# One decode block on one core: query 0's first 24 keys loaded into the values' buffer, ahead of the first weights

## The chip, the cores and the metric

The kernel runs on one core of a Trainium2 chip. A core has five engines that work side by side: TensorE (PE, matrix multiplies), VectorE (DVE), ScalarE (ACT), GpSimd (POOL) and SyncE (SP), which here does nothing but issue transfers. Sixteen transfer (DMA) engines carry data between memory and the core's own buffers. The metric is the time of one execution in microseconds (us), as the median of several runs. Before the change it is 1301.37 us over three runs (1301.36 to 1301.38).

## The reference

One token for each of two batch entries goes through attention over a cache of 8192 keys and values, and then through a gated layer without a nonlinearity:

```python
# B = 2, D = 448, H = 16 heads, Sk = 8192, Dh = 256, F = 1792
h  = x + attention(layernorm(x), k_cache, v_cache, wq, wo)
#    q = layernorm(x) @ wq, split by head;  scores = q . k * Dh**-0.5
#    p = softmax(scores);  o = p @ v;  attention = o @ wo
n  = layernorm(h)
h2 = h + ((n @ w_gate) * (n @ w_up)) @ w_down
```

All is float32. There are 32 queries (16 heads by two batch entries), and each has 8.39 MB of keys and as much of values that no other query reads.

## The kernel before

The 8192 keys of a query lie on 128 partitions as 64 keys of 256 numbers each ("j" from 0 to 63 in the code). A transfer of all keys of a query is 128 rows of 64 KB. The buffer `k_sb` (line 245) has 112 such key slots: even queries take slots 0 to 63 and odd ones 48 to 111 (`k_base`, line 276), so the two overlap in 16 slots. The buffer `v_sb` (line 246) has 64 slots and holds the values of one query at a time. Its last two slots hold the input x at the start (line 263).

For each query VectorE multiplies the keys with the query in place (`scores`, line 451, `tensor_mul`) and reduces every key to one score (`tensor_reduce`), in two parts: 16 keys first, and then 48. For query 0 the parts are other ones: `FIRST` (line 22) names keys 40 to 63 (the "first 24 keys") and then keys 0 to 39. The products of the first part go to the start of `v_sb` and not back to `k_sb` (line 459). So slots 48 to 63 of `k_sb` come free for query 1's keys as soon as that multiply is done. VectorE then takes the maximum of the scores, TensorE and ScalarE make the softmax, and TensorE multiplies it with the values (`mix`, line 496).

At the very start TensorE turns x around, a layer norm is made of it, and 16 multiplies of two passes each (32 in the trace, name `q_ps<-w_sb,xb`) give the queries of heads 0 and 1 out of the first weights. They come in four groups of eight passes. Behind each group ScalarE copies one query (`q<-q_ps,rstd`). VectorE's first multiply needs the query of the first group.

All large transfers are issued by SyncE, in program order, and each is held back until the place that it writes is free. A list of accesses by buffer and range (`_needs`, line 112) works out which engine has to be waited for. The order at the start is: the weights `d_w0` (line 303), query 0's keys 40 to 63 and then 0 to 39 (lines 304 and 305), query 1's keys, query 0's values, query 2's keys, further weights, query 1's values. Query 0's values need `v_sb`, so they wait for the reduction of the first 24 keys. Query 2's keys need slots 0 to 63, so they wait until query 0's keys and the first 16 keys of query 1 are reduced.

Of the kernel before, what the change touches and what calls it, by code (L numbers as in the profile page):

```python
# [10 lines left out]
B, D, H, SK, DH, F = 2, 448, 16, 8192, 256, 1792  # L11
# [10 lines left out]
FIRST = ((NJ - AHEAD, NJ), (0, NJ - AHEAD))  # L22
# [193 lines left out]
def decode_block(nc, x, k_cache, v_cache, w, wg, wu, wd, out):  # L216
# [3 lines left out]
    def sb(name, *shape):  # L220
        return nc.alloc_sbuf_tensor(name, list(shape), F32)[:]
# [9 lines left out]
    def dve(method, *args, **kw):  # L231
        put("DVE", method, *args, **kw)
# [13 lines left out]
    v_sb = sb("v_sb", P, NJ, DH)  # L246
# [19 lines left out]
    def keys(cache, i, lo, hi):  # L266
        h, b = divmod(i, B)
        return cache[b, h].rearrange("(p j) d -> p j d", p=P)[:, lo:hi, :]

    def load_keys(name, cache, i, lo, hi, buf, at, event=None):  # L270
        o.load(
            "SP", name, buffers[buf][:, at : at + hi - lo, :], keys(cache, i, lo, hi),
            writes=[(buf, at * DH, (at + hi - lo) * DH)], event=event,
        )

    def k_base(i):
        return i % 2 * (NJ - OVER)

    def load_k(i, lo=0, hi=NJ):
        load_keys(f"d_k_{i}_{lo}", k_cache, i, lo, hi, "k", k_base(i) + lo)  # L280
# [13 lines left out]
    def load_w(name, k, lo, hi, event=None):  # L294
        o.load("SP", name, w_sb[:, lo:hi], w[k][:, lo:hi], writes=[("w", lo, hi)], event=event)
# [4 lines left out]
    def wo_at(h):  # L300
        return 2 * WQ + h % 4 * WO

    load_w("d_w0", 0, 0, WQ)
    for lo, hi in FIRST:
        load_k(0, lo, hi)

    ident = sb("ident", P, P)
    put("POOL", "memset", ident, 0.0, w=["ident"])
# [77 lines left out]
    def q_at(h):  # L386
        return h % 2 * (1 + h // 2 % 2)

    for k in range(2):
        for b in range(B):  # L390
            for c in range(DC):
                at = c * 2 * DH + (k * DH if c < DC - 1 else 0)
# [5 lines left out]
            at = q_at(k)  # L398
# [44 lines left out]
    def score_parts(i):  # L443
        if i == 0:
            return list(FIRST)
        at = [(k - 1) % (NJ // HC) * HC if i % 2 == 0 else k * HC for k in range(NJ // HC)]
        if i in FINE:
            return [(lo, lo + HC) for lo in at]
        return [(at[0], at[0] + HC), (at[1], at[1] + NJ - HC)]

    def scores(i, part, between=None):
        h, b = divmod(i, B)
        s, name = s_t[i % 2], f"s{i % 2}"
        lo, hi = score_parts(i)[part]
        at = k_base(i) + lo
        kt = k_sb[:, at : at + hi - lo, :]
        qk, there = kt, ("k", at * DH, (at + hi - lo) * DH)
        if i == 0 and part == 0:
            qk, there = v_sb[:, : hi - lo, :], ("v", 0, (hi - lo) * DH)
        q, slot = qs[b], q_at(h)  # L460
        here = ("k", at * DH, (at + hi - lo) * DH)
        dve(
            "tensor_mul", qk, kt, q[:, slot, :][:, None, :].to_broadcast([P, hi - lo, DH]),
            r=[here, (f"q{b}", slot, slot + 1)], w=[there],
        )
        if between is not None:
            between()
        dve("tensor_reduce", s[:, lo:hi], qk, axis=AX.X, op=ALU.add, r=[there], w=[(name, lo, hi)])
# [143 lines left out]
    for n in range(NQ + 1):  # L612
        hp, at = divmod(n, 2 * B)
# [3 lines left out]
        if n < NQ:  # L617
            scores(n, 0, (lambda: softmax(n - 1)) if n > 0 else None)
        else:
            softmax(n - 1)  # L620
# [8 lines left out]
        if n % 8 == 1:  # L629
            k = n // 8 + 1  # L630
# [5 lines left out]
        if n == NQ:  # L636
            norm_last()
        else:
            for part in range(1, len(score_parts(n))):
                scores(n, part, norm_last if part == 1 else None)  # L640
# [25 lines left out]
    at = 0  # L666
# [191 lines left out]
```

## Time and profile before

| | |
|---|---|
| median of three runs | 1301.37 us |
| span of the profiled execution, first to last instruction | 1300.5 us |
| what the timed median has beyond that span | 0.9 us |
| VectorE busy | 1130.8 us (87%) |
| TensorE busy | 488.8 us (38%) |
| moved by the transfer engines | 561.45 MB, 432 GB/s over the span |
| chain that ended last | DMA 70%, DVE 29% |

The page gives no time of the profiled execution other than its span. The span leaves out what lies ahead of the first instruction and behind the last one. The chain that ended last is followed back from the last instruction, at each step to what released it. A transfer is listed by its issue, with the time until it has landed, which includes its wait in the queue behind earlier transfers.

### The profile page before, as it was taken

What the parts mean: (1) busy time and instruction counts of PE and PEld (TensorE: products, weight loads), DVE (VectorE), ACT (ScalarE), POOL (GpSimd) and SP (SyncE); (2) the same over time, 40 slices, a digit from 0 to 9 for tenths busy, and PEclk for the clock granted to TensorE, in tenths of its full rate; (3) what the DMA queues carried; (4) which work ended last, traced back from release to release, by engine and by line L of the source; (5) the groups of instructions that cost most, each with busy time, mean ns of one, the idle gap of its engine ahead of it and who ended that gap; (6) DMA issues with size and microseconds to landing.
All of it is one profiled execution on the core that took longest, in us unless ns stands there. A gap on an engine that the chain in (4) does not pass through costs nothing.

```text
span 1300.5 us, 6955 instructions
## 1 busy us (share of the span) xinstructions
PE 488.8 (38%) x2972; PEld 168.9 (13%) x2972; DVE 1130.8 (87%) x275; ACT 62.6 (5%) x184; POOL 1.4 (0%) x9
## 2 busy tenths in 40 slices
PE   3035422363331633215343063432424334243368
PEld 2011100120100201002101021010111001010113
DVE  7996988888988689888889868898888897889991
ACT  1000000000000000000000000000000000000000
POOL 0000000000000000000000000000000000000000
PEclk8566756686656766558666576665766667666578
DMA  9999999999999999999999999999999999999998
GB/s 414 423 434 448 424 437 431 427 441 423 448 424 435 448 423 443 427 439 429 435 435 423 433 448 423 448 424 443 427 443 427 423 436 445 426 438 429 435 433 374
DMA packets 12111, 561.45 MB, mean 432 GB/s; under 512 B 1602, under 2 KB 1732, under 8 KB 1988
## 3 DMA queue, kind: packets, MB, share of 16 engines
q1 hardware_dynamic: 12096, 561.30, 99.8%
q8 instruction: 6, 0.10, 0.0%
q14 instruction: 5, 0.04, 0.0%
q10 hardware_dynamic: 4, 0.00, 0.0%
HBM read 561.19 MB, written 0.11 MB: 432 GB/s over the span
## 4 chain that ended last, share of the span: by engine, by line
DMA 70%; DVE 29%; PE 0%; issue 0%; SPq 0%
DMA k_sb<-in_A_k_cache_dram 68%; DVE k_sb L229 14%; DVE s L229 14%; DMA k_sb<-in_wd_dram 2%; DVE nm L229 0%; PE y_ps L229 0%; SPq L176 0%; DVE m L229 0%; PE sm L229 0%; DVE v_sb L229 0%; DVE rl L229 0%
## 5 line engine op out<-in xcount | busy, mean ns | idle before, releaser
L229 DVE TENSOR_TENSOR k_sb<-k_sb,q 128x12288 f32<-128x12288 f32 (+2 forms) x67 | 549.6, 8203 | 130.3 <-DMA k_sb<-in_A_k_cache_dram 130.3
L229 DVE TENSOR_REDUCE s<-k_sb 128x48 f32<-128x12288 f32 (+2 forms) x67 | 549.3, 8198 | 0.2
L229 PE MATMUL o_ps<-v_sb,p 128*2 128x512 f32 x2000 | 288.2, 739 | 397.7 <-PEq L183 387.6
L229 PEld LDWEIGHTS o_ps<-v_sb,p 128*2 128x2 f32 x2000 | 53.7, 97 | 603.8 <-issue 591.3
L229 PE MATMUL sm<-nm,ones 1*128 1x1 f32 x64 | 16.6, 326 | 191.7 <-PEq L183 175.1
L229 PE MATMUL sm<-ident,m 128*1 128x128 f32 x32 | 10.9, 341 | 137.0 <-PEq L183 106.1
L229 PE MATMUL q_ps<-w_sb,xb 128*128 128x256 f32 (+1 forms) x172 | 59.3, 503 | 0.0
L229 ACT ACTIVATE o_sb<-o_ps 128x512 f32<-128x512 f32 x32 | 19.1, 597 | 703.9 <-PE o_ps L229 703.9
L229 PE MATMUL sm<-sel,o_sb 128*128 128x1 f32 x256 | 33.7, 253 | 25.8 <-PEq L183 22.9
L229 PE MATMUL acc_ps<-w_sb,oT 128*2 128x448 f32 x60 | 36.6, 749 | 15.9 <-PEq L183 11.0
L229 PEld LDWEIGHTS sm<-nm,ones 1*128 1x128 f32 x64 | 14.6, 283 | 201.2 <-issue 183.5
L229 PEld LDWEIGHTS sm<-sel,o_sb 128*128 128x128 f32 x256 | 31.8, 195 | 55.6 <-issue 48.2
L229 PEld LDWEIGHTS q_ps<-w_sb,xb 128*128 128x128 f32 x172 | 33.7, 200 | 30.0 <-issue 27.6
L229 PE MATMUL sm<-lsum,ones 128*128 128x1 f32 x64 | 17.5, 342 | 26.0 <-PEq L183 23.1
L229 ACT ACTIVATE nb<-sm 128x1 f32<-128x1 f32 x32 | 5.5, 171 | 395.7 <-PE sm L229 395.7
L229 PEld LDWEIGHTS sm<-ident,m 128*1 128x1 f32 x32 | 2.6, 81 | 149.8 <-issue 115.3
L229 PEld LDWEIGHTS sm<-lsum,ones 128*128 128x128 f32 x64 | 15.6, 303 | 28.0 <-issue 24.7
L229 ACT ACTIVATE q<-q_ps,rstd 128x512 f32<-128x512 f32 (+1 forms) x18 | 11.5, 640 | 71.9 <-PE q_ps L229 71.9
L229 PE MATMUL o_ps<-k_sb,p 128*2 128x512 f32 x48 | 9.3, 934 | 6.1 <-DMA k_sb<-in_A_v_cache_dram 6.1
L229 ACT ACTIVATE p<-s,nb 128x64 f32<-128x64 f32 x32 | 11.1, 347 | 1.0
L229 DVE TENSOR_TENSOR v_sb<-k_sb,q 128x6144 f32<-128x6144 f32 x1 | 6.6, 6557 | 4.8 <-DMA k_sb<-in_A_k_cache_dram 4.8
L229 PE MATMUL q_ps<-k_sb,xr 128*32 128x256 f32 (+3 forms) x96 | 10.0, 506 | 1.6 <-DMA k_sb<-in_B_w_gate_dram 1.6
(79 smaller groups left out, 85.1 us busy)
## 6 DMA issues: line engine op xcount, KB each, us to landing
v_sb<-in_A_v_cache_dram SPq DMA_DIRECT2D x4, 4096.0 KB, 30.5
w_sb<-in_w_dram SPq DMA_DIRECT2D x3, 3584.0 KB, 37.8
v_sb<-in_A_v_cache_dram SPq DMA_DIRECT2D x1, 6144.0 KB, 24.3
k_sb<-in_A_k_cache_dram SPq DMA_DIRECT2D x1, 5120.0 KB, 24.6
v_sb<-in_A_v_cache_dram SPq DMA_DIRECT2D x2, 2048.0 KB, 27.3
k_sb<-in_A_v_cache_dram SPq DMA_DIRECT2D x1, 4096.0 KB, 35.3
k_sb<-in_B_w_gate_dram SPq DMA_DIRECT2D x1, 3136.0 KB, 32.4
k_sb<-in_A_k_cache_dram SPq DMA_DIRECT2D x1, 3072.0 KB, 11.6
```

What stands on the lines that cost most here:

```text
L229: o.put(engine, lambda: f(*args, **kw), r, w, mark, event)
```

## The change

The first 24 keys of query 0 are loaded to the start of `v_sb`, in a transfer of its own, `d_k_first`, which is issued ahead of the first weights. The other 40 keys go to `k_sb` as before. VectorE's first multiply reads the keys in `v_sb` and writes its products over them; `here` names the range that it reads, and `there` the range that it writes.

```diff
@@ -300,9 +300,9 @@
+    load_keys("d_k_first", k_cache, 0, *FIRST[0], "v", 0)
     load_w("d_w0", 0, 0, WQ)
-    for lo, hi in FIRST:
-        load_k(0, lo, hi)
+    load_k(0, *FIRST[1])
@@ -455,10 +455,12 @@
         at = k_base(i) + lo
         kt = k_sb[:, at : at + hi - lo, :]
         qk, there = kt, ("k", at * DH, (at + hi - lo) * DH)
+        here = there
         if i == 0 and part == 0:
-            qk, there = v_sb[:, : hi - lo, :], ("v", 0, (hi - lo) * DH)
+            kt = v_sb[:, : hi - lo, :]
+            qk, here = kt, ("v", 0, (hi - lo) * DH)
+            there = here
         q, slot = qs[b], q_at(h)
-        here = ("k", at * DH, (at + hi - lo) * DH)
```

SyncE's queue at the head of the program, with what each transfer waits for in brackets (128x6144 are 24 keys, 128x10240 are 40, 128x16384 are all 64; w_sb takes weights):

```order
-L176 DMA w_sb<-in_w_dram 128x1792 [waits barrier_Pool_Activation_PE_DVE_SP_release]
-L176 DMA k_sb<-in_A_k_cache_dram 128x6144
+L176 DMA v_sb<-in_A_k_cache_dram 128x6144 [waits barrier_Pool_Activation_PE_DVE_SP_release]
+L176 DMA w_sb<-in_w_dram 128x1792
 L176 DMA k_sb<-in_A_k_cache_dram 128x10240
-L176 DMA k_sb<-in_A_k_cache_dram 128x16384 [waits DVE]
+L176 DMA k_sb<-in_A_k_cache_dram 128x16384
 L176 DMA v_sb<-in_A_v_cache_dram 128x16384 [waits DVE,PE]
 L176 DMA k_sb<-in_A_k_cache_dram 128x16384 [waits DVE]
```

The first two transfers have changed places, and query 1's keys, the fourth, no longer wait for VectorE, since nothing of query 0 lies in slots 48 to 63 of `k_sb`.

VectorE at its first multiply, again with the waits (d_k_0_40 and d_k_first are the transfers of the first 24 keys, ACT is the copy of the first query):

```order
 L229 RECIPROCAL rstd<-std 128x2 [waits ACT]
 L229 COPY pair<-ident 2x32
-L229 TENSOR_TENSOR v_sb<-k_sb,q 128x6144 [waits d_k_0_40,ACT]
+L229 TENSOR_TENSOR v_sb<-v_sb,q 128x6144 [waits d_k_first,ACT]
 L229 TENSOR_REDUCE s<-v_sb 128x24 [waits DVE]
 L229 TENSOR_TENSOR k_sb<-k_sb,q 128x10240 [waits d_k_0_0]
```

No instruction of VectorE has moved; the multiply reads another buffer and waits for another transfer.

## Rows read from the trace of the kernel before

**Rows 1.** The page: its span, and the queue of all large transfers (packets, MB, share)

```profile
span 1300.5 us, 6955 instructions
...
q1 hardware_dynamic: 12096, 561.30, 99.8%
```

**Rows 2.** VectorE's waits: us in total, times, longest us

```profile
DVE k_sb L229 <- DMA k_sb<-in_A_k_cache_dram: 130.3, 29, 12.1
```

**Rows 3.** Busy time by window, all engines, the middle of the span

```profile
core 0: us, PE busy (x) PEld busy (x) DVE busy (x) ACT busy (x) POOL busy (x), PEclk, DMA share, GB/s
...
900.00:1200.00 300.00, 112.63 (x646) 36.76 (x646) 268.32 (x56) 13.36 (x41) 0.00 (x0) 0.65 1.00 434
```

**Rows 4.** Transfers issued between 0 and 20 us: KB, us to landing

```profile
k_sb<-in_A_k_cache_dram SPq DMA_DIRECT2D x1, 3072.0 KB, 11.6
w_sb<-in_w_dram SPq DMA_DIRECT2D x1, 896.0 KB, 4.8
```

**Rows 5.** SyncE in order of time, 0 to 60 us: start, us, transfer

```profile
0.73 0.38 SPq L176 DMA_DIRECT2D w_sb<-in_w_dram  x1
1.17 18.57 SPq L176 DMA_DIRECT2D k_sb<-in_A_k_cache_dram  x3
26.07 0.33 SPq L176 DMA_DIRECT2D v_sb<-in_A_v_cache_dram  x1
57.05 0.33 SPq L176 DMA_DIRECT2D k_sb<-in_A_k_cache_dram  x1
```

**Rows 6.** Transfers between 17 and 30 us: code reads, and values with time to landing

```profile
q8 instruction: 1, 0.02, 0.4%
...
v_sb<-in_A_v_cache_dram SPq DMA_DIRECT2D x1, 38.8
```

**Rows 7.** VectorE in order of time, 12 to 58 us, idle time before in brackets

```profile
12.83 6.56 DVE L229 TENSOR_TENSOR v_sb<-k_sb,q 128x6144 f32<-128x6144 f32 x1 [4.83 <-DMA k_sb<-in_A_k_cache_dram]
19.42 6.55 DVE L229 TENSOR_REDUCE s<-v_sb 128x24 f32<-128x6144 f32 x1
26.24 10.82 DVE L229 TENSOR_TENSOR k_sb<-k_sb,q 128x10240 f32<-128x10240 f32 x1 [0.27 <-DMA k_sb<-in_A_k_cache_dram]
...
52.62 4.40 DVE L229 TENSOR_REDUCE s<-k_sb 128x16 f32<-128x4096 f32 x1
```

**Rows 8.** Order of time, 6 to 18 us: TensorE's query multiplies, ScalarE's first copy

```profile
7.30 9.25 PE L229 MATMUL q_ps<-w_sb,xb 128*128 128x256 f32 x32
...
11.10 0.47 ACT L229 ACTIVATE q<-q_ps,rstd 128x256 f32<-128x256 f32 x1 [1.85 <-PE q_ps L229]
```

**Rows 9.** Order of time, TensorE's weight loads: the first of query 0's values

```profile
64.94 0.14 PEld L229 LDWEIGHTS o_ps<-v_sb,p 128*2 128x2 f32 x8 [10.25 <-issue]
```

**Rows 10.** Windows of `q_ps` alone, no POOL column: first and third query group

```profile
7.20:11.10 3.90, 3.80 (x9) 3.15 (x10) 0.00 (x0) 0.00 (x1) 1.00 1.05 454
...
13.10:14.80 1.70, 1.70 (x9) 1.50 (x9) 0.00 (x0) 0.47 (x1) 1.00 0.95 410
```

**Rows 11.** Instructions that read `w_sb`, 0 to 60 us: min/median/max ns

```profile
L229 PE MATMUL q_ps<-w_sb,xb x32: 379/380/774, 7.3 to 16.2; 128*128 128x256 f32 x32
```

**Rows 12.** Windows as in rows 3, where query 0's values end

```profile
62.00:62.50 0.50, 0.00 (x0) 0.00 (x0) 0.50 (x1) 0.00 (x0) 0.00 (x0) 0.50 0.00 0
62.50:63.00 0.50, 0.00 (x0) 0.00 (x0) 0.50 (x1) 0.00 (x0) 0.00 (x0) 0.50 3.94 1704
```

**Rows 13.** Windows as in rows 3, the start

```profile
1.00:1.50 0.50, 0.00 (x0) 0.00 (x0) 0.15 (x3) 0.20 (x1) 0.34 (x2) 1.00 0.00 0
1.50:2.00 0.50, 0.00 (x0) 0.00 (x0) 0.32 (x2) 0.50 (x1) 0.50 (x3) 1.00 1.11 179
2.00:3.00 1.00, 0.01 (x1) 0.01 (x1) 0.88 (x3) 0.58 (x1) 0.14 (x1) 1.00 0.71 165
```

**Rows 14.** VectorE in order of time, 83 to 132 us: the next two queries begin

```profile
84.17 4.43 DVE L229 TENSOR_TENSOR k_sb<-k_sb,q 128x4096 f32<-128x4096 f32 x1 [1.04 <-DMA k_sb<-in_A_k_cache_dram]
...
131.25 4.43 DVE L229 TENSOR_TENSOR k_sb<-k_sb,q 128x4096 f32<-128x4096 f32 x1 [12.04 <-DMA k_sb<-in_A_k_cache_dram]
```

## The prediction

> **What bounds the kernel now.** I began with the page's queue table [rows 1]: the reader is to see that SyncE's one queue keeps the sixteen transfer engines busy for 99.8% of a span of 1300.5 us. Next the waits of VectorE [rows 2]: 130.3 us in 29 waits, all for keys, so VectorE is the faster partner and is held back by transfers, never the other way round for long. A stretch in the middle [rows 3] gives the pace: 434 GB/s at a share of 1.00. The whole traffic of 561.3 MB [rows 1] takes 1293 us at that pace, which leaves 7 us of the span for the first bytes and the last landing. The kernel is bound by its bytes, and an edit can move the time in only two ways: it changes how soon the engines reach full pace, or it lets their queue run empty once. Both can only happen in the first 65 us, so there I read the issues and landings [rows 4 to 6] and VectorE's instructions [rows 7].
>
> The sum is made against the span of 1300.5 us; the timed median of 1301.37 us is 0.9 us more, and I add that to each result.
>
> **The order of the first two transfers.** Before, the weights (896 KB) are issued at 0.73 and land 4.8 us later, at 5.5; the 24 keys (3072 KB) follow at 1.17 and land 11.6 later, at 12.77 [rows 4, 5]. The second transfer alone took 12.77 - 5.5 = 7.2 us, which is 3.15 MB at 434 GB/s: they are served one after the other. Now the keys go first and land near 5.5 + (7.2 - 2.1) = 10.6 (2.1 us is 0.92 MB at 434 GB/s), and the weights come in as the sum of the same bytes, at 12.77.
>
> **The first query.** Before, TensorE's query multiplies began at 7.30, right behind the layer norm, and the first query was ready to be copied at 11.10, 3.80 us later [rows 8]; the copy took 0.47. VectorE then waited for keys until 12.83 [rows 7]. Now TensorE waits for the weights. What follows a landing starts at once: 0.06 us behind the keys (12.77 to 12.83), 0.07 behind the first values (issued 26.07, 38.8 us to landing, so 64.87; weights of the matmul at 64.94) [rows 5 to 7, 9]. So TensorE starts at 12.85, the first query is copied at 16.65, and VectorE starts at 16.65 + 0.47 + 0.06 = 17.2, which is 4.4 us later than before. The keys that arrive 2 us sooner win nothing, since the query is now what comes last.
>
> The 3.80 us is a slow pace: the third group, with the same work, took 1.70 us [rows 10] (a group is four multiplies of two passes each; the x9 counts one that reaches over the edge of the window). If the first group ran at that pace, VectorE would be only 2.3 us late; if every pass took the longest seen, 774 ns [rows 11], eight passes would need 6.2 us and VectorE would be 6.8 late. I take 3.80, since the row is the same group after the same small matmuls.
>
> Both stretches are listed with a granted clock of 1.00, that is 2.4 GHz [rows 10], so the row does not put the difference down to the clock. The Trainium skill ("TensorE: Matmul & The Clock Gate", section "Part 1: The HAM clock gate") says that an idle TensorE falls to half rate and that the matmuls just after a pause run slow. Here the change makes TensorE pause from the layer norm to 12.85, and by that rule the first group stays slow and VectorE is 4.4 late, where the fast pace would make it 2.3; the end of the kernel is the same by either, only the reserve named below differs.
>
> **What VectorE's lateness reaches.** The first multiply and reduction take 6.56 and 6.55 us as before (the multiply now reads and writes the values' buffer in place; an in-place multiply of 10,240 elements took 10.82 us, the same 1.06 ns each) [rows 7]. The next multiply had waited 0.27 us for keys [rows 7], which now have landed long before; so from there VectorE is 4.4 - 0.27 = 4.1 us late. Three issues on SyncE hang on it:
>
> - Query 1's keys. Before they waited for the first multiply and went out near 1.17 + 18.57 = 19.7 [rows 5]; now they wait for nothing. The 40 keys ahead of them landed only at 26.2 (VectorE's wait for them ends at 26.24 [rows 7]), so the queue was not empty then, and the earlier issue is worth 0.
> - The first values go out at 26.07 + 4.4 = 30.4. Query 1's keys keep the queue busy until about 43 (17.7 MB at 434 GB/s is 41 us, after a start of 2 to 3), so this costs 0.
> - Query 2's keys went out at 57.05 [rows 5], behind the reduction of query 1's first 16 keys (52.62 + 4.40 [rows 7]). Now 57.05 + 4.1 = 61.2. This is the place that decides. What is queued ahead ends with the first values: 26.1 MB, 60.1 us at 434 GB/s, behind a start of 2.5. So most engines come free near 62.6, and the windows show the batch that follows: 1704 GB/s between 62.5 and 63.0, nothing in the half microsecond ahead [rows 12]; that is 13 of the 16 engines beginning a 64 KB row together. The slowest engine goes on to 64.87. From an issue to its first bytes the start shows 0.73 to a point between 1.5 and 2.0, so 0.8 to 1.3 us [rows 5, 13]. 61.2 plus that is 62.0 to 62.5: the new keys arrive in the queue 0.1 to 0.6 us before it is empty. Cost 0, but the reserve, which was 4.2 to 4.7 us, is nearly spent.
>
> The Trainium skill ("DMA: Bandwidth & Descriptors", section "Latency and other measured facts") puts the first byte at about 0.6 us, less than the 0.8 to 1.3 us that the row gives; by its figure the reserve would be 0.8 us, by the row 0.1 to 0.6, and the row decides.
>
> Behind it nothing is near. Query 2's keys land at 84.1, and VectorE had been waiting 1.04 us for them; for query 3's it waited 12.04 us, until 131.25 [rows 14]. A lateness of 4.1 becomes 3.1 at the first and nothing at the second. From then on each step is released by transfers, as before. At the other end nothing is moved.
>
> **The start.** The first bytes come between 1.5 and 2.0; until 3.0 only 0.25 MB moved [rows 13], which is 0.6 us of work in 1.0 to 1.5 us, so 0.4 to 0.9 us is lost while the engines get going on short rows of 7 KB. With rows of 24 KB in front the loss may shrink to nothing or be the same; it could also grow by as much. I take a gain of 0.2, near the same, because a first delay would be paid once either way. The bounds are a gain of 0.9 and a loss of 0.9. One engine also carries a read of code, 16 KB, in this stretch [rows 6], and so ends 1 to 2 us behind the rest; if it falls on another moment, the last landing can shift by some tenths.
>
> **Sum:** 1300.5 + 0 (issue of query 1's keys) + 0 (first values) + 0 (query 2's keys) - 0.2 (start) = 1300.3 span, 1301.2 us timed. A repeat of the kernel holds within 0.01 us, but I call no change what lies within 0.2%, or 2.6 us.
>
> **Rivals.**
> First, slower: query 2's keys come after the queue is empty. For it speaks how thin the reserve is; against it, that the lateness was taken from rows of the same instructions. Every microsecond beyond 4.2 to 4.7 us of lateness leaves the engines without work for that long, and lost transfer time is never won back in a kernel bound by bytes. With the longest passes, 6.8 - 0.3 = 6.5 us late, the gap is 1.8 to 2.3 us on most engines: 1303.0 to 1303.5 us. To pass 0.2% VectorE would have to be over 7 us late. The slowest engine, which sets the end, would see no gap before 64.87, so even that price may not be paid in full.
> Second, faster: the larger rows in front bring the engines to full pace at once and 0.9 us is saved: 1300.5 us. For it, the slow first 1.5 us of the rows; against it, that nothing shows row size to be the cause. More than 0.9 us is not there to win, as every later microsecond is at full pace.
> Third, the change does not do what it says: the transfers are shared between the two, the weights land well before 12.77, and VectorE is late by little or even early. The 7.2 us of the second transfer at full pace speaks against it. VectorE's gain would end in longer waits for keys: 1301.3 us.
>
> **How the numbers follow.** The forecast has 0.78, the first rival 0.12, the second 0.06, the third 0.04. The forecast and the third lie within 0.2%, as do the prices worked out for the other two; I leave 0.05 for a gap over 2.6 us and 0.03 for a gain over 2.6 us that no row shows. So no change has 0.92. The range runs from the full gain at the start, 1300.5, to a gap of about 1 us, 1302.4.
>
> **What would show it.** VectorE's first multiply begins at 17.2 with an idle time ended by ScalarE's query, not by keys; the query multiplies begin at 12.85 and still take 3.8 us for the first group; query 1's keys are issued before 3; the first values at 30.4, query 2's keys at 61.2, and the batch near 62.6 is still there without a gap; VectorE's waits for keys in their own buffer fall from 130.3 us by 0.27 + 1.04 + 3.1, to 125.9. I am wrong if the share of the transfer engines drops near 62 to 65 us, or if the landings differ by more than 1 us at 130.

## The result, and the profile after

The changed kernel takes 1303.60 us (median of 13 runs, 1302.56 to 1304.68), the kernel before 1301.37 us (13 runs, 1301.24 to 1301.73). The ratio is 1.0017, with a 95% interval of 1.0009 to 1.0025. So it is slower, by 2.2 us. That is less than the 0.2% that I call no change, but it lies clear of zero, and the time lies outside the range of 1300.5 to 1302.4.

The steps up to VectorE's lateness came out nearly as worked out. The transfers issued in the first 20 us (KB, us to landing), which answer to [rows 4]:

```profile
v_sb<-in_A_k_cache_dram SPq DMA_DIRECT2D x1, 3072.0 KB, 9.6
w_sb<-in_w_dram SPq DMA_DIRECT2D x1, 896.0 KB, 11.3
```

The keys land at 0.73 + 9.6 = 10.3 and the weights at 1.17 + 11.3 = 12.5 (I had 10.6 and 12.77). TensorE and then ScalarE in order of time, for [rows 8]:

```profile
12.54 9.91 PE L229 MATMUL q_ps<-w_sb,xb 128*128 128x256 f32 x32 [5.10 <-DMA w_sb<-in_w_dram]
```

```profile
16.36 0.47 ACT L229 ACTIVATE q<-q_ps,rstd 128x256 f32<-128x256 f32 x1 [7.11 <-PE q_ps L229]
```

The first group took 16.36 - 12.54 = 3.82 us, the slow pace again. The trace's records of the granted clock begin only at 11.56 us before and at 18.11 here. Up to about there a pass of these multiplies takes 634 ns in the median, and from there on 380. So the 1.00 that [rows 10] list for the first group belongs to a stretch without a record and says nothing against the clock as the cause; no row here shows the clock of that stretch.

VectorE in order of time, for [rows 7, 14]:

```profile
16.86 6.56 DVE L229 TENSOR_TENSOR v_sb<-v_sb,q 128x6144 f32<-128x6144 f32 x1 [8.87 <-ACT q L229]
23.46 6.55 DVE L229 TENSOR_REDUCE s<-v_sb 128x24 f32<-128x6144 f32 x1
29.93 10.82 DVE L229 TENSOR_TENSOR k_sb<-k_sb,q 128x10240 f32<-128x10240 f32 x1
...
56.30 4.40 DVE L229 TENSOR_REDUCE s<-k_sb 128x16 f32<-128x4096 f32 x1
...
86.72 4.42 DVE L229 TENSOR_TENSOR k_sb<-k_sb,q 128x4096 f32<-128x4096 f32 x1
...
132.92 4.42 DVE L229 TENSOR_TENSOR k_sb<-k_sb,q 128x4096 f32<-128x4096 f32 x1 [11.16 <-DMA k_sb<-in_A_k_cache_dram]
```

The first multiply waits for ScalarE's query until 16.86 and not for keys. Query 3's keys, the last row, are multiplied at 132.92, where before it was 131.25: 1.7 us of the loss are there by then, although VectorE still waits 11.16 us for those keys. So transfers lost the time, and VectorE did not. SyncE's issues, for [rows 5]:

```profile
1.17 0.42 SPq L176 DMA_DIRECT2D w_sb<-in_w_dram  x1
1.64 0.95 SPq L176 DMA_DIRECT2D k_sb<-in_A_k_cache_dram  x2
30.10 0.33 SPq L176 DMA_DIRECT2D v_sb<-in_A_v_cache_dram  x1
60.73 0.33 SPq L176 DMA_DIRECT2D k_sb<-in_A_k_cache_dram  x1
```

Query 2's keys go out at 60.73 (forecast 61.2, before 57.05). Now the windows where the queue changes over to them, for [rows 12] (the last two columns are the share of the 16 engines and GB/s; a transfer's row is counted where it begins):

```profile
62.00:62.50 0.50, 0.00 (x0) 0.00 (x0) 0.50 (x1) 0.00 (x0) 0.00 (x0) 0.50 0.00 0
62.50:63.00 0.50, 0.00 (x0) 0.00 (x0) 0.50 (x1) 0.00 (x0) 0.00 (x0) 0.50 2.69 1049
63.00:63.50 0.50, 0.00 (x0) 0.00 (x0) 0.50 (x1) 0.00 (x0) 0.00 (x0) 0.50 0.89 262
63.50:64.00 0.50, 0.00 (x0) 0.00 (x0) 0.50 (x1) 0.00 (x0) 0.00 (x0) 0.50 0.92 262
64.00:64.50 0.50, 0.00 (x0) 0.00 (x0) 0.50 (x1) 0.00 (x0) 0.00 (x0) 0.50 1.32 393
...
65.00:65.50 0.50, 0.00 (x0) 0.02 (x1) 0.50 (x1) 0.00 (x0) 0.00 (x0) 0.50 2.77 918
```

Before, the last of these windows was:

```profile
65.00:65.50 0.50, 0.50 (x4) 0.08 (x8) 0.50 (x1) 0.00 (x0) 0.00 (x0) 0.50 3.63 1573
```

A row of 64 KB in half a microsecond is 131 GB/s. So 8 rows begin by 63.0, where before 13 did, and 2, 2 and 3 more trickle in up to 64.5. The share tells how long such a row takes: 16 engines times 0.5 us times the share, divided by the rows. That is 2.42 us a row before (3.94 x 8 / 13). Here it is 2.7 us on average for the first eight and 3.5 to 3.7 us for the late seven (0.89 x 8 / 2, 0.92 x 8 / 2, 1.32 x 8 / 3). The late engines begin up to 1.9 us late (64.5 less 62.6) and lose another 1.1 to 1.3 us on their first row. The engines that began on time are slowed as well, on their next row: the seven rows that begin between 65.0 and 65.5 take 3.2 us each (2.77 x 8 / 7), where before twelve took 2.42 there (3.63 x 8 / 12). The 22 rows of the windows from 62.5 to 65.5 take 15.5 us more than at 2.42 us each (8.59 x 8 - 22 x 2.42), which is 1.0 us for each of the sixteen engines. So more than half of the 1.7 us is slow rows, and by this estimate the late begins have the smaller part.

Two waits of VectorE, for [rows 2]:

```profile
DVE k_sb L229 <- DMA k_sb<-in_A_k_cache_dram: 127.9, 27, 12.1
...
DVE v_sb L229 <- ACT q L229: 8.9, 1, 8.9
```

The span is 1302.6 us and the pace in the middle still 434 GB/s:

```profile
900.00:1200.00 300.00, 111.26 (x644) 35.40 (x644) 268.35 (x54) 13.05 (x39) 0.00 (x0) 0.66 1.00 434
```

### The profile page after: what moved, and what is told of

Same layout as the page of the kernel before. It is cut to its first block, busy times and chain, and to the rows that moved or that the text cites. A ratio compares the mean times of both kernels' runs of the same rounds, so it can differ in the third digit from the quotient of the medians.

```text
span 1302.6 us, 6955 instructions
## 1 busy us (share of the span) xinstructions
PE 487.2 (37%) x2972; PEld 168.8 (13%) x2972; DVE 1130.6 (87%) x275; ACT 62.6 (5%) x184; POOL 1.4 (0%) x9
## 4 chain that ended last, share of the span: by engine, by line
DMA 67%; DVE 32%; PE 0%; issue 0%; SPq 0%; ACT 0%
DMA k_sb<-in_A_k_cache_dram 64%; DVE s L229 16%; DVE k_sb L229 15%; DMA k_sb<-in_wd_dram 2%; DMA w_sb<-in_w_dram 1%; DVE v_sb L229 1%; DVE nm L229 0%; PE q_ps L229 0%; PE y_ps L229 0%; DVE m L229 0%; SPq L176 0%; ACT q L229 0%; DVE rl L229 0%; PE sm L229 0%
## 5 line engine op out<-in xcount | busy, mean ns | idle before, releaser
L229 DVE TENSOR_TENSOR k_sb<-k_sb,q 128x12288 f32<-128x12288 f32 (+2 forms) x67 | 549.6, 8202 | 127.9 <-DMA k_sb<-in_A_k_cache_dram 127.9
L229 DVE TENSOR_TENSOR v_sb<-v_sb,q 128x6144 f32<-128x6144 f32 x1 | 6.6, 6559 | 8.9 <-ACT q L229 8.9
```

The lines of the kernel that those rows point to most:

```text
L229: o.put(engine, lambda: f(*args, **kw), r, w, mark, event)
```

## The experiments

The theory was: the loss is paid where query 2's keys reach a queue that holds less than 2 us of work. The rivals were other places of the change: query 1's keys queued without a wait, the multiply in place, the new order at the start, and where the read of code falls.

**The order undone.** The keys stay in the values' buffer, behind the weights:

```diff
+    load_w("d_w0", 0, 0, WQ)
     load_keys("d_k_first", k_cache, 0, *FIRST[0], "v", 0)
-    load_w("d_w0", 0, 0, WQ)
```

> The change without its new order: the first 24 keys still go to the values' buffer, but behind the first weights, as before the change. VectorE then starts its first multiply near 12.8 us again and query 2's keys are issued near 57. Theory (the loss comes from query 2's keys reaching the queue with only 1.7 us of work left in it): no loss, 1301.0 to 1301.6. Rival (the loss comes from another place of the change: query 1's keys queued without a wait, or keys multiplied in place in the values' buffer): the loss stays, about 1303.5.

Measured: 1301.43 us (before, beside it: 1301.44; ratio 1.0, 0.9991 to 1.001). The loss is gone, and query 2's keys are issued at 56.94. The buffer, the multiply in place and the early issue of query 1's keys are all still there, so none of them makes the loss. The order remains.

**The lateness alone, in the kernel before.** Behind the first reduction:

```diff
         dve("tensor_reduce", s[:, lo:hi], qk, axis=AX.X, op=ALU.add, r=[there], w=[(name, lo, hi)])
+        if i == 0 and part == 0:
+            dve("tensor_reduce", s[:, lo : lo + 15], qk[:, :15, :], axis=AX.X, op=ALU.add,
+                r=[there], w=[(name, lo, lo + 15)])
```

> The kernel before, with one more reduction on VectorE behind query 0's first part (15 of its 24 keys reduced a second time into the same scores, about 4.1 us), so that query 2's keys are issued near 60.9 as in the changed kernel (60.73), with the old order of transfers. Theory: the whole loss returns without the change, 1303 to 1304.3, and the first rows of query 2's keys take over 3 us instead of 2.42. Rival (the new order at the start, or where the read of code falls, makes one engine late): as before, 1301.2 to 1301.7.

Measured: 1303.71 us (1302.85 to 1304.68; ratio 1.0017, 1.0008 to 1.0026). The whole loss comes back with the old order and the old buffer. Its windows at the same place:

```profile
62.50:63.00 0.50, 0.00 (x0) 0.00 (x0) 0.50 (x1) 0.00 (x0) 0.00 (x0) 0.50 2.77 1180
63.00:63.50 0.50, 0.00 (x0) 0.00 (x0) 0.50 (x1) 0.00 (x0) 0.00 (x0) 0.50 0.45 131
63.50:64.00 0.50, 0.00 (x0) 0.00 (x0) 0.50 (x1) 0.00 (x0) 0.00 (x0) 0.50 0.95 262
64.00:64.50 0.50, 0.00 (x0) 0.00 (x0) 0.50 (x1) 0.00 (x0) 0.00 (x0) 0.50 1.24 393
```

The picture is that of the changed kernel: 9 rows on time, 6 late ones at 3.3 to 3.8 us on average by window.

**The changed kernel with an earlier issue.** Query 2's keys in two transfers, of which the first 48 keys need only query 0's slots:

```diff
-            load_k(n + 1)
+            if n == 1:
+                load_k(2, 0, NJ - OVER)
+                load_k(2, NJ - OVER, NJ)
+            else:
+                load_k(n + 1)
```

> The changed kernel, with query 2's keys loaded in two transfers: keys 0 to 47, whose slots are free when query 0 is reduced (near 51.7), and keys 48 to 63, issued at 60.7 as now. Theory: the queue never gets short, the loss goes, 1300.9 to 1301.5 (the start is 0.3 us sooner than before by the landings of query 0's keys). Rival (code read, order at the start): 1303 to 1304.

Measured: 1301.65 us (1301.27 to 1301.96; ratio 1.0001, 0.9992 to 1.001). VectorE is as late as in the changed kernel, the order is the changed one, and the loss is gone. SyncE shows the first part at 51.55:

```profile
51.55 9.43 SPq L176 DMA_DIRECT2D k_sb<-in_A_k_cache_dram  x2
61.02 0.45 SPq L176 DMA_DIRECT2D w_sb<-in_w_dram  x1
```

**The changed kernel with more work in the queue.** The second block of weights ahead of query 2's keys:

```diff
+        if n == 1:
+            load_w("d_w_1", 1, 0, WALL, event("e_w", n))
         if n + 1 < NQ:
             load_k(n + 1)
...
-        if n % 8 == 1:
+        if n % 8 == 1 and n > 1:
```

> The changed kernel, with the second block of weights (3584 KB, 8.4 us of transfer) issued ahead of query 2's keys and not behind them. Query 2's keys are issued at 60.7 as now, but with some 10 us of work left in the queue in place of 1.7. Theory: the loss goes, 1300.9 to 1301.6; VectorE waits some 8 us longer for query 2's keys. Rival (the time of that issue in itself, VectorE's lateness or the start): 1303 to 1304.

Measured: 1301.66 us (1301.35 to 1301.86; ratio 1.0002, 0.9992 to 1.0011). SyncE, and then VectorE:

```profile
30.32 0.43 SPq L176 DMA_DIRECT2D w_sb<-in_w_dram  x1
60.57 0.33 SPq L176 DMA_DIRECT2D k_sb<-in_A_k_cache_dram  x1
```

```profile
92.48 4.43 DVE L229 TENSOR_TENSOR k_sb<-k_sb,q 128x4096 f32<-128x4096 f32 x1 [5.83 <-DMA k_sb<-in_A_k_cache_dram]
```

The keys are issued at 60.57, just as late, and it costs nothing, since 8.4 us of weights lie ahead of them. So it is not the time of the issue that counts, but how much work the queue holds then. VectorE's wait of 5.83 us for them (forecast some 8) is free too. Both cures end 0.2 us over the kernel before and a little above their expected ranges (1301.65 against at most 1301.5, and 1301.66 against at most 1301.6). So no gain at the start shows, though intervals of 0.1% (1.3 us) to either side are too wide to exclude the 0.2 us that I gave to it.

**How much work is needed.** The kernel before with other lengths of the added reduction (8, 12, 19 or 24 keys in place of 15; for 36 one reduction of 24 and one of 12).

> The kernel before with 8 of query 0's first 24 keys reduced twice on VectorE (2.2 us more, 0.27 of it in a wait that goes), so query 2's keys are issued near 58.9, some 3.7 us ahead of the point (62.6) where most engines finish the first values. Theory A (a transfer that arrives within some 2 to 3 us of the end of the queue already costs, because its first rows start late and run slow): no loss or up to 0.5, 1301.3 to 1301.9. Theory B (only an empty queue costs, first bytes 1.0 us behind the issue): no loss, 1301.4.

> As the last, with 12 keys reduced twice (3.3 us): query 2's keys are issued near 60.0, 2.6 us ahead of 62.6. Theory A: a part of the loss, 1301.8 to 1303. Theory B: no loss, 1301.4.

> As the last, with all 24 keys reduced twice (6.55 us): query 2's keys are issued near 63.3, 0.7 us after most engines finish the first values, so the queue is empty for all but the slowest engine. Theory A: the loss of the run with 15 keys (2.3 us) and the 2.4 us of further lateness, 1305.5 to 1306.5. Theory B: 6.3 us late less 4.5 us of reserve, 1303.0 to 1303.5.

> The kernel before with 19 of query 0's first 24 keys reduced twice (5.2 us), query 2's keys issued near 61.7, 0.9 us ahead of the point where most engines run dry (62.6): between the runs with 15 keys (60.68, 1303.7) and 24 keys (62.97, 1303.9). Theory (the whole step of 2.3 us is paid as soon as the keys are issued with less than about 2 us of work left, and stays level until the queue is truly empty): 1303.4 to 1304.3. Rival (arriving while engines are still busy is the worst case, worse than an empty queue): over 1304.5.

> The kernel before with 36 key reductions more (24 and 12, 9.8 us), query 2's keys issued near 66.2, 3.3 us later than in the run with 24 keys and 3.6 us after most engines run dry. Theory (past the step each microsecond of lateness costs one): 1303.9 + 3.3 = 1307.2, 1306.5 to 1307.8. Rival (the slowest engine, 1.6 us behind the rest, or later slack gives a part back): 1305 to 1306.2.

In the third column 62.6 us is the end of the queue that the prediction worked out for most engines.

| run | query 2's keys issued | us ahead of 62.6 | median us | over before beside it | ratio, 95% interval |
|---|---|---|---|---|---|
| before | 57.05 | 5.5 | 1301.37 | | |
| 8 keys | 58.76 | 3.8 | 1301.32 | 0.0 | 1.0 (0.9991 to 1.0009) |
| 12 keys | 59.83 | 2.8 | 1302.09 | 0.7 | 1.0007 (0.9998 to 1.0016) |
| 15 keys | 60.68 | 1.9 | 1303.71 | 2.3 | 1.0017 (1.0008 to 1.0026) |
| changed kernel | 60.73 | 1.9 | 1303.60 | 2.2 | 1.0017 (1.0009 to 1.0025) |
| 19 keys | 61.70 | 0.9 | 1303.27 | 1.9 | 1.0014 (1.0005 to 1.0023) |
| 24 keys | 62.97 | -0.4 | 1303.89 | 2.5 | 1.002 (1.001 to 1.0029) |
| 36 keys | 66.56 | -4.0 | 1307.37 | 6.0 | 1.0044 (1.003 to 1.0058) |

Each issue time is from one profile. With 3.8 us of work ahead nothing is lost. With 2.8 us the 11 runs scatter from 1301.29 to 1303.79, so this is the edge, and the interval of its ratio does not exclude no change. From 1.9 us ahead to 0.4 behind the loss lies level at about 2 us; the intervals do not tell these four runs apart. Behind that it is about one for one, by two runs: 3.59 us later costs 3.48. Both theories on the form were partly wrong. Theory B, only an empty queue costs, has no room for the 2.3 us at 60.68. Theory A let the loss grow from there and expected 1305.5 to 1306.5 for 24 keys, where it is 1303.89, above the 1303.0 to 1303.5 of theory B too. The rival for 19 keys, that a busy queue is worse than an empty one (over 1304.5), is not borne out; the level step was expected at 1303.4 to 1304.3 there, and 1303.27 lies just below.

The run with 12 keys shows slow rows without late ones:

```profile
62.50:63.00 0.50, 0.00 (x0) 0.00 (x0) 0.50 (x1) 0.00 (x0) 0.00 (x0) 0.50 4.45 1704
```

As many rows begin here as before, 13, but they take 2.74 us each (4.45 x 8 / 13) in place of 2.42. With 8 keys 15 rows begin there and take 2.43.

With 24 keys most engines really are idle. Its windows:

```profile
63.00:63.50 0.50, 0.00 (x0) 0.00 (x0) 0.50 (x1) 0.00 (x0) 0.00 (x0) 0.50 0.00 0
63.50:64.00 0.50, 0.00 (x0) 0.00 (x0) 0.50 (x1) 0.00 (x0) 0.00 (x0) 0.50 1.97 655
64.00:64.50 0.50, 0.00 (x0) 0.00 (x0) 0.50 (x1) 0.00 (x0) 0.00 (x0) 0.50 3.42 1180
64.50:65.00 0.50, 0.13 (x4) 0.14 (x8) 0.50 (x1) 0.00 (x0) 0.00 (x0) 0.50 0.74 262
```

Sixteen rows begin within 0.5 to 2.0 us of the issue at 62.97, most of them between 0.5 and 1.5, and take 3.0 to 3.2 us on average (1.97 x 8 / 5, 3.42 x 8 / 9, 0.74 x 8 / 2) in place of 2.42. So an empty queue costs the delay to the first bytes and 0.5 to 0.7 us on the first row. In the changed kernel the issue came at 60.73 and its last rows begin only after 64.0, at least 3.3 us later.

## Why the prediction was wrong

The step that failed is the third of VectorE's lateness: "the new keys arrive in the queue 0.1 to 0.6 us before it is empty. Cost 0". The place and the times were right: the issue came at 60.73, against 61.2 worked out. The rule that set the price, that only an empty queue costs, was wrong: the cost there was not 0 but 2.2 us, with some 2 us of work left. Two things in it were wrong.

- I took the time from an issue to the first bytes anywhere (0.8 to 1.3 us) as the time until all engines have work. With a busy queue the last engines got their first rows over 3 us after the issue.
- I left out that rows run slow behind such an issue, and by the estimate from the windows this is the larger part in the changed kernel. In [rows 13] I had found 0.4 to 0.9 us lost after the first bytes, but booked it to the start alone; no run shows whether the two have the same cause. The engine need not have stood idle for it: the rows of the run with 12 keys, and the second rows of the engines that began on time, are slow too.

The runs put the reserve's end elsewhere than at 4.2 to 4.7 us of lateness: the level loss is paid at 3.7 us late (60.73 instead of 57.05), and nothing at 1.7 (58.76). The straight part gives the whole delay: 1307.37 is 6.0 us over before, and 66.56 less 6.0 is 60.6, which is 2.0 us ahead of 62.6. The windows with 24 keys divide such a price into the wait for the first bytes, 0.5 to 2.0 us, and the slow first row. The Trainium skill ("DMA: Bandwidth & Descriptors", section "Anatomy of one DMA — SWDGE (gpsimd) path") also has about 2.0 us, as the fixed cost of a transfer by another path, but puts most of it behind the last byte. What is lost here lies at the first rows, so the likeness of the two figures shows nothing.

Point by point: the two transfers are served one after the other (right). The query is what comes last, at the slow pace of 3.8 us (right; 3.82). VectorE's lateness of 4.4, then 4.1 us (right in kind; 16.86 - 12.83 = 4.0 and 60.73 - 57.05 = 3.7). Query 1's keys and the first values cost 0 (right, by the run with the order undone and the two cures). The gain of 0.2 at the start: none shows in the runs. The waits for keys of 125.9 us: 127.9, higher by the lost transfer time. The first rival was the true case, and it had 0.12; its price at this lateness, by its own rule, would still have been nothing. Both signs of being wrong came: too little begins near 62 to 65 us, and the keys land 1.7 us later at 131.

Two smaller readings were off, and neither made the loss. The 0.9 us between span and time joined the median with the span of another execution; in the profiled run of the changed kernel it is 1.3 (1303.89 against 1302.6). And repeats of the kernel before do not hold within 0.01 us: 13 of them spread over 0.5.

## What to carry to other kernels

Where transfers bound the kernel, look for the one place where the queue of transfers is shortest, and count an edit's lateness against the work left in it then. Here 3.8 us of work was enough and 2.8 us was the edge, though the first bytes follow an issue within 1.3 us; with 2 us left about the same price was paid as with a queue just empty. The cures are cheap, and both worked here: issue any transfer that is free to go ahead of the one that has to wait, or split off the part whose place is free.

## What the hardware showed that I had not expected

A transfer issued to busy engines at the end of their queue fared as badly as one issued to idle ones: 2.3 us at 60.68 and 2.5 us at 62.97. Its late rows of 64 KB took 3.5 to 3.7 us on average, longer than the 3.0 to 3.2 us behind an empty queue, and the last of them began over 3 us after the issue. Slow rows also come without late ones (2.74 us with 12 keys). Why the engines get their first rows so unevenly, and why rows run slow behind such an issue, was not settled.

The runs also scatter more when the queue is short but not empty: 1302.56 to 1304.68 for the changed kernel, against 1301.24 to 1301.73 before and 1303.59 to 1304.24 with 24 keys.
